# An attention, Fourier and feed-forward kernel: the first layer of the feed-forward over 512 tokens at once, the inner width in two halves

## The chip, the cores and the metric

The kernel runs on one core of one Trainium2 chip. The metric is the device time of one execution in microseconds (us), lower is better; the figure given for a kernel is the median of several runs. Engines are called PE (TensorE, matmuls), DVE (VectorE), ACT (ScalarE), POOL (GpSimd) and SP (SyncE, which issues the transfers).

## The reference

Eight batches, eight heads, 576 tokens, head width 64, so 512 channels; the inner width of the feed-forward is 2048.

```python
scores = q @ k.T / 8                                   # per batch and head, 576 x 576
scores = where(0 <= i - j < 128, scores - slope[h] * abs(i - j), -1e9)
x = softmax(scores) @ v                                # heads joined: (8, 576, 512)
mixed = real(fft(fft(x, axis=1), axis=2))              # over tokens, then channels
u = x + mixed
un = (u - mean(u)) / sqrt(var(u) + 1e-6)               # over channels
out = u + relu(un @ w_ch1) @ w_ch2                     # 512 -> 2048 -> 512
```

## The kernel before, in words

One function records the whole program. Every step is a small closure that is put into a heap, `queue`, at a planned time (`put`, or `after` for a time relative to the step that runs now); a last loop takes them out in the order of these times and records their instructions. The constants at the top (L44 to L60) are such times, in units in which a batch takes 24 and a pair of heads 6. A scheduler behind the recording then fixes the final order on each engine from the tiles' dependences and the buffers. A batch has four pairs of heads, so there are 32 pairs, called the first to the 32nd here.

**Attention.** For a pair, `scores` (L406) multiplies the keys by the queries into `sp` banks (L422). A float16 product is done as three: high by high, low by high, high by low, and 64 rows of TensorE are used by one head, the other 64 by the other head. DVE adds bias and mask from the scaled table `rg` (L434) and takes the row's largest value; ACT takes the exponential (L183, as all steps put by `after` carry the line of its lambda). Batches 0 and 1 (`NF` = 2) stay in float32: `turn` transposes P on TensorE (L466) and `values` multiplies (L488). Later batches split P in a high and a low half (`halves`, L448) and transpose it by a DMA (`flip`, L457), and `values` takes three products (L493 to L495). `weigh` divides by the row sums into `X` (L507 to L511). `warm` (L340, L342) records dummy matmuls that nobody reads, `SPL[p]` of them after each turn of pair p, and `N0` at the start (L338).

**Scales.** `batch_scales` (L274) loads a batch's q, k and v once more to find its scales, and makes the table `rg` = scale x `rel_sb` (L317, ACT, 128 x 1152, two buffers).

**Fourier.** `fourier(b, ...)` folds the rows of `X` (L555 to L604, DVE and ACT), multiplies by the cosine and sine tables over tokens (L619), then over channels (L637, L655), and `norm` (L715) normalizes, splits `un` in two float16 halves and transposes each token tile into `uT` with a DMA (`turned`, L749). `uT` holds two token tiles of 128 tokens, in three buffers; a batch has four full token tiles in two of them, and 64 tokens more, which for two batches together make one tile `ut`.

**Feed-forward.** `ffn(b)` (L765) is a generator; `step` (L835) runs it from one `yield` to the next at planned times, beginning at `forward_of(b)`. It goes over parts: two of two token tiles (256 columns), and in odd batches the `ut` tile (128 columns). A part runs the whole first layer: two inner groups f of 128 at a time share one 512-column bank `fp`, each with 12 matmuls (four channel groups, three products; L783). ACT takes the Relu into the high half of `hbuf` (L788), DVE the rest into the low half (`lower`, L758), which gives the bank back. Then the second layer (L799): for each token tile 48 matmuls of 512 columns (16 groups f, three products), and `joined` (L762) adds the result to `X` on DVE; the tile is sent out. Banks for `fp` come from `take` (two of three in turn, all three once `late` is set). The first weight, w1, and the second, w2, are split at the start by `weights` (L192, L245 to L249) into `wall`.

Of the kernel before, what the change touches and what calls it, by code (L numbers as in the profile page):

```python
# [43 lines left out]
LB, LC = 2, 5.046  # L44
E0 = 17.576
W1A, N0 = 1.058, 20
WL = (-2.569, 0.042)
PL, VL = 8.703, 2.996
PQ, T2, DF1, ST1, F1 = 0.911, 0.0, 29.452, 49.362, 0.9
SPL = (5, 6, 5, 5, 1, 1, 1, 1)  # L50
FL, SA, SD, SB, SE = 2.073, 16.745, 0.696, 24.163, 1.152
DFT = 29.394
START = 48.566
PACE, T1 = (0.443, 0.427), 13.679
GAP = 0.73
SLOW = 1.386
W2A, W2D, W2B, W2E = 16.635, 0.564, 21.18, 0.402
W1D, W1B, W1E = 0.379, 11.323, 0.508
F0 = 6.021
# [24 lines left out]
def attn_fft_ffn_kernel(  # L84
# [189 lines left out]
    def batch_scales(b, t0, dt):  # L274
# [28 lines left out]
        def scale():  # L303
            r = small.tile([128, 3], F32, name="r")
            root_inv(r, box["sums"])
            give(("scale", b))
            sc = small.tile([128, 8], F32, name="sc", bufs=3)
            V.tensor_scalar_mul(sc[:, 0:1], r[:, 0:1], 2.0 ** -58)
            V.tensor_scalar_mul(sc[:, 1:3], r[:, 1:3], 2.0 ** -51)
            V.scalar_tensor_tensor(sc[:, 3:4], sc[:, 0:1], 8.0, sc[:, 1:2], ALU.mult, ALU.mult)  # L310
            gi = small.tile([128, 8], F32, name="gi")
            V.reciprocal(gi[:, 0:1], sc[:, 3:4])
            nsl = small.tile([128, 12], F32, name="nsl")
            V.tensor_scalar(nsl[:, 0:8], slope_sb[:, 0:8], gi[:, 0:1], None, ALU.mult)
            V.tensor_scalar(nsl[:, 8:12], slope_sb[:, 8:12], sc[:, 0:1], None, ALU.mult)
            rg = att.tile([128, 1152], BF16, name="rg", bufs=2)
            A.activation(rg, rel_sb, AF.Copy, scale=sc[:, 3:4])  # L317
            x_scales(sc, gi, r[:, 2:3])
            scs[b] = sc, nsl, rg
# [54 lines left out]
    def convert(p, what):  # L374
# [7 lines left out]
        sc, nsl, rg = scs[b]  # L382
# [23 lines left out]
    def scores(p, i):  # L406
# [19 lines left out]
        for e in range(2):  # L426
            h = 2 * j + e
            nb = small.tile([128, 5], F32, name="nb", bufs=6)
# [30 lines left out]
    def turn(p, i, e):  # L459
# [11 lines left out]
        after(GAP, warm, upper, SPL[p])  # L471
# [243 lines left out]
    def norm(b, of, t1):  # L715
        tiles = of()
        n = len(tiles)
        if n == 2:
            uT = dft.tile([128, 2, 4, 256], F16, name="uT", bufs=3)
        else:  # L720
            assert (1, 7) in ready
            uT = wall[1][:, 8, 0:512].bitcast(F16).rearrange("p (e c t) -> p e c t", e=2, c=4)
        uTs[b].append(uT)
        ag = small.tile([128, 4, 2], F32, name="ag")
# [12 lines left out]
        def scaled(i):  # L737
# [7 lines left out]
            after(0.5 * f, turned, dst, both)  # L745

        def turned(dst, both):
            ready.add((b, id(uT)))
            nc.sync.dma_start_transpose(dst, both)  # L749
# [15 lines left out]
    def ffn(b):  # L765
# [3 lines left out]
        parts = [(uTs[b][i], 256, [X[:, XS[2 * i]], X[:, XS[2 * i + 1]]], 4 * b + 2 * i) for i in range(2)]  # L769
        if b % 2 == 1:  # L770
            parts.append((uTs[b][2], 128, [uts[b // 2]], 4 * B + b // 2))
        for uT, n, tiles, slot in parts:
            per = 512 // n
            hh = []
            assert (b, id(uT)) in ready
            for f0 in range(0, 16, per):
# [3 lines left out]
                for i in range(per):  # L780
# [4 lines left out]
                    if i == per // 2 - 1:  # L785
                        yield
# [3 lines left out]
                for i in range(per):  # L790
                    hh.append(ht[:, :, i * n:(i + 1) * n])
                yield
            for i, t in enumerate(tiles):
                key = ("second", b, slot, i)
                op = take(key, "fp")
                for f in range(16):
                    assert (1, f // 2) in ready
                    for p, (a, e) in enumerate(((0, 0), (0, 1), (1, 0))):
                        T.matmul(op, hh[f][:, a, i * 128:(i + 1) * 128], w2_ap(e, f),  # L799
                                 start=(f == 0 and p == 0), stop=(f == 15 and p == 2))  # L800
                    if f % 2 == 1 and f < 15:
                        yield
                after(0.15, joined, key, t, op)
                after(0.4, nc.sync.dma_start, out=ov[slot + i], in_=t)
# [162 lines left out]
```

## Time and profile before

| | us |
|---|---|
| median of 3 runs | 1052.02 |
| lowest and highest | 1051.59, 1053.05 |
| the profiled execution, whole | 1052.83 |
| its span, first to last instruction | 1051.0 |
| PE busy | 1027.8 |
| DVE busy | 701.1 |
| ACT busy | 582.2 |

The profile shows one execution. Busy time of an engine is the time in which it had an instruction at work; idle time is put down to whatever released the engine afterwards. [...] In rows of the timeline a run of like instructions is one row with its count (x24), and consecutive matmuls overlap, so a row's length is a little more than the distance to the start of the next.

### The profile page before, as it was taken

The page shows a single profiled execution, that of the slowest core. Times are in us where ns is not written, and L with a number is a line of the kernel's source. Part 1 is how long each engine was busy: PE and PEld are TensorE (multiplying, and loading weights), DVE is VectorE, ACT ScalarE, POOL GpSimd, SP SyncE. Part 2 cuts the span into 40 slices and gives each one's busy share as a digit, 9 for nine tenths or more (in the row PEclk, how much of TensorE's full clock was granted, in tenths as well). Part 3 has the DMA queues.
Part 4 walks back from the last instruction along what each step waited for, and adds up shares of the span by engine and source line. Part 5 has one row for each costly group of instructions (what it writes and reads, how often), then busy time and mean ns, then how long its engine had stood idle before and what let it go on. Part 6 is the DMA issues. An engine that isn't in the chain of part 4 may idle for free.

```text
span 1051.0 us, 24075 instructions
## 1 busy us (share of the span) xinstructions
PE 1027.8 (98%) x9214; PEld 721.6 (69%) x9214; DVE 701.1 (67%) x2073; ACT 582.2 (55%) x1388; POOL 77.4 (7%) x211
## 2 busy tenths in 40 slices
PE   8998999999999999999999999999999999999998
PEld 5885785575758677676767676776667775857656
DVE  5889769878676858696875858696866726532111
ACT  6887877667556646676555656665545512331100
POOL 0000003101010002110010012110000000000000
PEclk9996989999999999999999999999999999999999
DMA  9971356927752554636762475637322410030000
GB/s 365 357 237 37 106 125 171 206 64 145 172 132 67 135 116 117 154 71 143 167 144 54 110 151 116 157 67 155 72 64 34 91 35 11 12 70 1 21 11 21
DMA packets 191507, 117.82 MB, mean 112 GB/s; under 512 B 154400, under 2 KB 164128, under 8 KB 191392
## 3 DMA queue, kind: packets, MB, share of 16 engines
q1 hardware_dynamic: 190816, 114.84, 44.9%
q8 instruction: 72, 1.18, 0.5%
q10 hardware_dynamic: 576, 1.45, 0.4%
q14 instruction: 43, 0.35, 0.1%
HBM read 70.63 MB, written 9.44 MB: 76 GB/s over the span
## 4 chain that ended last, share of the span: by engine, by line
PE 83%; DVE 8%; DMA 3%; ACT 3%; issue 2%; POOL 0%; SPq 0%; ACTq 0%; DVEq 0%; POOLq 0%
PE fp L799 32%; PE fp L783 31%; PE sp L422 6%; PE pv L488 3%; PE pd L619 3%; DMA pt<-P 2%; DVE P L434 1%; PE sp L466 1%; PE pv L342 1%; PE pv L493 1%; PE pd L655 1%; PE pv L495 1%; PE pv L494 1%; DVE hbuf L758 1%; PE fp L225 1%
## 5 line engine op out<-in xcount | busy, mean ns | idle before, releaser
L799 PE MATMUL fp<-wall,hbuf 128*128 128x512 f16 x1728 | 393.2, 379 | 0.7 <-DVE hbuf L758 0.7
L783 PEld LDWEIGHTS <-wall 128*128 128x128 f16 x3840 | 337.6, 98 | 43.1 <-issue 4.3
L783 PE MATMUL fp<-uT,wall 128*128 128x256 f16 x3072 | 358.3, 273 | 0.4 <-DVE hbuf L758 0.4
L799 PEld LDWEIGHTS <-hbuf 128*128 128x128 f16 x1728 | 162.9, 98 | 183.2 <-issue 3.7
L788 ACT ACTIVATE hbuf<-fp 128x512 f16<-128x512 f32 x144 | 84.3, 589 | 194.0 <-PE fp L783 194.0
L183 ACT ACTIVATE P<-P,nb 128x256 f32<-128x256 f32 x320 | 142.0, 479 | 79.6 <-DVE nb L434 79.1
L758 DVE SCALAR_TENSOR_TENSOR hbuf<-fp,hbuf 128x512 f16<-128x512 f32 x144 | 98.4, 685 | 87.9 <-ACT hbuf L788 87.2
L434 DVE CUSTOM_DVE_ANT_0 P<-sp,rg,nsl 128x256 f32<-128x256 f32 x240 | 97.4, 449 | 26.2 <-PE sp L422 24.7
L183 DVE SCALAR_TENSOR_TENSOR P<-P 128x256 f16<-128x256 f32 x240 | 88.9, 390 | 31.9 <-ACT P L448 29.7
L448 ACT ACTIVATE P<-P 128x256 f16<-128x256 f32 x240 | 86.7, 382 | 14.0 <-DMA pt<-P 11.5
L422 PE MATMUL sp<-kk,qq 64*128 64x256 f16 (+4 forms) x880 | 89.1, 289 | 1.5 <-DVE m L173 1.0
L296 ACT ACTIVATE wall<-wall 128x512 f32<-128x512 f32 (+2 forms) x90 | 54.1, 602 | 22.2 <-POOL mx L295 6.6
L762 DVE SCALAR_TENSOR_TENSOR X<-fp,misc,X 128x512 f32<-128x512 f32 x32 | 23.7, 742 | 54.1 <-PE fp L799 54.1
L288 POOL COPY wall<-nb 1x1 f32<-1x1 f32 x75 | 34.2, 459 | 339.0 <-DVE nb L434 225.1
L493 PE MATMUL pv<-vhs,pt 128*128 128x65 f16 x432 | 54.1, 195 | 4.7 <-DMA pt<-P 2.5
L494 PE MATMUL pv<-vl,pt 128*128 128x64 f16 x432 | 54.2, 193 | 0.0
L495 PE MATMUL pv<-vhs,pt 128*128 128x65 f16 x432 | 53.7, 193 | 0.0
L493 PEld LDWEIGHTS <-pt 128*128 128x128 f16 x432 | 41.0, 98 | 14.2 <-issue 4.1
L422 PEld LDWEIGHTS <-qq 64*128 64x128 f16 (+1 forms) x720 | 29.9, 99 | 24.1 <-issue 18.8
L494 PEld LDWEIGHTS <-pt 128*128 128x128 f16 x432 | 40.4, 99 | 7.3
L783 PE MATMUL fp<-wall,wall 128*128 128x128 f16 x768 | 45.0, 219 | 0.0
L488 PEld LDWEIGHTS pv<-vr,pt 128*128 128x128 f32 x288 | 39.1, 207 | 7.3 <-PE pv L342 4.2
(160 smaller groups left out, 1231.5 us busy)
## 6 DMA issues: line engine op xcount, KB each, us to landing
qr<-q_dram SPq DMA_DIRECT2D x32, 304.0 KB, 3.3
hbuf<-w_dram SPq DMA_DIRECT2D x16, 512.0 KB, 7.1
out_dram<-X SPq DMA_DIRECT2D x32, 256.0 KB, 2.5
wall<-v_dram SPq DMA_DIRECT2D x30, 256.0 KB, 2.9
vr<-v_dram SPq DMA_DIRECT2D x24, 320.0 KB, 3.8
kr<-k_dram SPq DMA_DIRECT2D x24, 289.0 KB, 3.5
wall<-q_dram SPq DMA_DIRECT2D x24, 256.0 KB, 3.1
wall<-k_dram SPq DMA_DIRECT2D x24, 256.0 KB, 2.9
```

Source lines behind the costliest of these rows:

```text
L183: put(now[0] + dt, lambda: f(*a, **kw))
L422: T.matmul(sp[e][:m, col:col + n], qq[h, c0:c0 + m], keys(kk[h], ti), start=(x == 0), stop=(x == len(prods) - 1))
L434: V.tensor_tensor_reduce(pt[:m, 0:n], sp[e][:m, col:col + n], tab[:m, pc:pc + n], mul, 3.0e38, ALU.add, ALU.min, nb[:m, ti:ti + 1])
L448: A.activation(hi, P32, AF.Copy, scale=2.0 ** 14)
L488: T.matmul(pv[:, ti], pt[:, col:col + 128], ops[p][2][:, e, vc], start=first, stop=last)
L493: T.matmul(pv[:, ti], ph, vh[:, e, vc], start=first, stop=False)
L494: T.matmul(pv[:, ti, 0:D], ph, vl[:, e, vc], start=False, stop=False)
L495: T.matmul(pv[:, ti], pl, vh[:, e, vc], start=False, stop=last)
L758: V.scalar_tensor_tensor(ht[:, 1], fp, 0.0, ht[:, 0], ALU.max, ALU.subtract)
L783: T.matmul(fp[:, i * n:(i + 1) * n], w1_ap(e, c, f0 + i), uT[:, j, c, 0:n], start=(c == 0 and p == 0), stop=(c == 3 and p == 2))
L788: A.activation(ht[:, 0], fp, AF.Relu)
L799: T.matmul(op, hh[f][:, a, i * 128:(i + 1) * 128], w2_ap(e, f), start=(f == 0 and p == 0), stop=(f == 15 and p == 2))
```

## The change

Three things. First, the first layer of a batch takes all four token tiles at once, so one inner group f fills a 512-column bank by itself, in 12 matmuls of 512 columns. `uT` now has 512 columns and two buffers, and the first layer needs all four transposed tiles. Second, the inner width is halved: eight groups f go through the first layer and then, for all four tiles, through the second (24 matmuls a tile), and then the other eight. Each token tile is therefore added into `X` twice, and sent out after the second time. The part of 128 columns stays as it was. Third, the table `rg` is made by a step of its own just before the batch's first scores and has one buffer. Besides, `nb` has four buffers instead of six, the count of dummies is given for each turn, and the planned times are set anew.

```diff
@@ -41,22 +41,23 @@
 TGRP = ((0, 1), (2, 3), (4,))
 
 
-LB, LC = 2, 5.046
-E0 = 17.576
-W1A, N0 = 1.058, 20
-WL = (-2.569, 0.042)
-PL, VL = 8.703, 2.996
-PQ, T2, DF1, ST1, F1 = 0.911, 0.0, 29.452, 49.362, 0.9
-SPL = (5, 6, 5, 5, 1, 1, 1, 1)
-FL, SA, SD, SB, SE = 2.073, 16.745, 0.696, 24.163, 1.152
-DFT = 29.394
+LB, LC = 2, 5.066
+E0 = 7.777
+W1A, N0 = 1.854, 21
+WL = (-2.569, 0.408)
+PL, VL = 7.761, 2.996
+PQ, T2, DF1, ST1, F1 = 0.754, -0.085, 28.727, 45.662, 0.9
+SPL = ((5, 2, 6, 7, 5, 5), (6, 6, 6, 6, 6, 6), (5, 5, 5, 4, 5, 5), (3, 5, 5, 5, 5, 5), (3, 1, 1, 1, 1, 1), (1, 1, 1, 0, 1, 1), (2, 1, 1, 1, 0, 2), (1, 1, 1, 3, 1, 0))
+RG = 0.2
+FL, SA, SD, SB, SE = 2.073, 16.545, 0.661, 23.561, 1.211
+DFT = 29.51
 START = 48.566
-PACE, T1 = (0.443, 0.427), 13.679
+PACE, T1 = (0.443, 0.497), 13.94
 GAP = 0.73
-SLOW = 1.386
-W2A, W2D, W2B, W2E = 16.635, 0.564, 21.18, 0.402
-W1D, W1B, W1E = 0.379, 11.323, 0.508
-F0 = 6.021
+SLOW = 1.35
+W2A, W2D, W2B, W2E = 16.635, 0.584, 20.304, 0.402
+W1D, W1B, W1E = 0.362, 11.211, 0.508
+F0 = 10.277
 SW = 184
 
 
@@ -313,10 +314,15 @@
             nsl = small.tile([128, 12], F32, name="nsl")
             V.tensor_scalar(nsl[:, 0:8], slope_sb[:, 0:8], gi[:, 0:1], None, ALU.mult)
             V.tensor_scalar(nsl[:, 8:12], slope_sb[:, 8:12], sc[:, 0:1], None, ALU.mult)
-            rg = att.tile([128, 1152], BF16, name="rg", bufs=2)
-            A.activation(rg, rel_sb, AF.Copy, scale=sc[:, 3:4])
             x_scales(sc, gi, r[:, 2:3])
-            scs[b] = sc, nsl, rg
+            scs[b] = sc, nsl
+
+        def table():
+            rg = att.tile([128, 1152], BF16, name="rg", bufs=1)
+            A.activation(rg, rel_sb, AF.Copy, scale=scs[b][0][:, 3:4])
+            scs[b] += rg,
+
+        put(begin_of(4 * b) - RG, table)
 
         put(t0 - 2.5 * dt, begin)
         x = 0
...
@@ -468,7 +474,7 @@
         pt = pts[p, i, e] = att.tile([128, 448], F32, name="pt", bufs=6)
         A.activation(pt[:, :col], tp[:, :col], AF.Copy)
         upper = pt.bitcast(BF16).rearrange("p (x e) -> p x e", e=2)[:, :, 1]
-        after(GAP, warm, upper, SPL[p])
+        after(GAP, warm, upper, SPL[p][2 * i + e])
 
     def values(p, i, e):
         b, j = divmod(p, 4)
@@ -715,12 +721,17 @@
     def norm(b, of, t1):
         tiles = of()
         n = len(tiles)
-        if n == 2:
-            uT = dft.tile([128, 2, 4, 256], F16, name="uT", bufs=3)
-        else:
+        o = 256 * len(uTs[b])
+        if n == 1:
             assert (1, 7) in ready
             uT = wall[1][:, 8, 0:512].bitcast(F16).rearrange("p (e c t) -> p e c t", e=2, c=4)
+        elif o:
+            uT = uTs[b][0]
+        else:
+            uT = dft.tile([128, 2, 4, 512], F16, name="uT", bufs=2)
         uTs[b].append(uT)
+        if n == 2:
+            uT = uT[:, :, :, o:o + 256]
         ag = small.tile([128, 4, 2], F32, name="ag")
         rstd = small.tile([128, 4], F32, name="rstd")
         nmr = small.tile([128, 4], F32, name="nmr")
@@ -742,10 +753,10 @@
             A.activation(both[:, 0:512], tiles[i], AF.Identity, scale=s, bias=o)
             after(0.3 * f, V.tensor_tensor, both[:, 512:1024], un, both[:, 0:512], ALU.subtract)
             dst = uT[:, :, :, i * 128:(i + 1) * 128].rearrange("p e c t -> p (e c) t")
-            after(0.5 * f, turned, dst, both)
-
-        def turned(dst, both):
-            ready.add((b, id(uT)))
+            after(0.5 * f, turned, dst, both, i)
+
+        def turned(dst, both, i):
+            ready.add((b, o, i))
             nc.sync.dma_start_transpose(dst, both)
 
         for i in range(n):
@@ -766,14 +777,16 @@
         if b:
             late.append(b)
         X = Xs[b]
-        parts = [(uTs[b][i], 256, [X[:, XS[2 * i]], X[:, XS[2 * i + 1]]], 4 * b + 2 * i) for i in range(2)]
+        parts = [(uTs[b][0], 512, [X[:, i] for i in XS], 4 * b, h) for h in range(2)]
         if b % 2 == 1:
-            parts.append((uTs[b][2], 128, [uts[b // 2]], 4 * B + b // 2))
-        for uT, n, tiles, slot in parts:
+            parts.append((uTs[b][2], 128, [uts[b // 2]], 4 * B + b // 2, None))
+        for uT, n, tiles, slot, h in parts:
             per = 512 // n
-            hh = []
-            assert (b, id(uT)) in ready
-            for f0 in range(0, 16, per):
+            fs = range(16) if h is None else range(8 * h, 8 * h + 8)
+            hh = {}
+            for o, i in ((0, 0), (0, 1), (256, 0), (256, 1)) if n == 512 else ((512, 0), ):
+                assert (b, o, i) in ready
+            for f0 in fs[::per]:
                 assert (0, (f0 + per - 1) // 2) in ready
                 key = ("first", b, slot, f0)
                 fp = take(key, "fp")
@@ -782,26 +795,27 @@
                         for p, (e, j) in enumerate(((0, 0), (0, 1), (1, 0))):
                             T.matmul(fp[:, i * n:(i + 1) * n], w1_ap(e, c, f0 + i), uT[:, j, c, 0:n],
                                      start=(c == 0 and p == 0), stop=(c == 3 and p == 2))
-                    if i == per // 2 - 1:
-                        yield
+                        if (i * 4 + c + 1) * 2 == per * 4:
+                            yield
                 ht = next(hslots)
                 A.activation(ht[:, 0], fp, AF.Relu)
                 after(0.2, lower, key, ht, fp)
                 for i in range(per):
-                    hh.append(ht[:, :, i * n:(i + 1) * n])
+                    hh[f0 + i] = ht[:, :, i * n:(i + 1) * n]
                 yield
             for i, t in enumerate(tiles):
-                key = ("second", b, slot, i)
+                key = ("second", b, slot, i, h)
                 op = take(key, "fp")
-                for f in range(16):
+                for f in fs:
                     assert (1, f // 2) in ready
                     for p, (a, e) in enumerate(((0, 0), (0, 1), (1, 0))):
                         T.matmul(op, hh[f][:, a, i * 128:(i + 1) * 128], w2_ap(e, f),
-                                 start=(f == 0 and p == 0), stop=(f == 15 and p == 2))
-                    if f % 2 == 1 and f < 15:
+                                 start=(f == fs[0] and p == 0), stop=(f == fs[-1] and p == 2))
+                    if f % 2 == 1 and f != fs[-1]:
                         yield
                 after(0.15, joined, key, t, op)
-                after(0.4, nc.sync.dma_start, out=ov[slot + i], in_=t)
+                if h != 0:
+                    after(0.4, nc.sync.dma_start, out=ov[slot + i], in_=t)
                 yield
```

The order of the instructions on each engine follows from the planned times. At three places it now reads as follows. In the rows, `vr`, `qq`, `kk` are the values, queries and keys of a pair, `pt` the transposed P, `wall` the weights, `hbuf` the inner activations, `fh` and `abcd` the folded rows of the Fourier step.

PE where the feed-forward of batch 0 begins, before:

```order
L342 LDWEIGHTS pt
L342 MATMUL pv<-pt 128x184
L488 MATMUL pv<-vr,pt 128x65 x2
L466 MATMUL sp_2157<-ident,P 128x128 x2
L783 LDWEIGHTS wall_112
L783 MATMUL fp<-uT,wall_112 128x256
```

and now:

```order
L494 MATMUL pv<-vr,pt 128x65 x2
L472 MATMUL sp_2042<-ident,P 128x128 x2
...
L494 MATMUL pv<-vr,pt 128x65 x3
...
L494 MATMUL pv<-vr,pt 128x65 x4
L348 LDWEIGHTS pt
L348 MATMUL pv<-pt 128x184
L494 MATMUL pv<-vr,pt 128x65 x2
L796 LDWEIGHTS wall_112
L796 MATMUL fp<-uT,wall_112 128x512
```

A turn (L466, now L472) stood directly ahead of the feed-forward; now nine more value matmuls and dummies (L348) stand between the two.

DVE about the first score step of the ninth pair (L434, now L440), before, where the fold of batch 1 begins some 40 rows further on:

```order
L511 TENSOR_TENSOR X<-pv,ri 128x5x64
L249 SCALAR_TENSOR_TENSOR wall_113<-wall_113,misc 128x1024
L267 TENSOR_SCALAR sc<-m_2109 128x1
L758 SCALAR_TENSOR_TENSOR hbuf<-fp,hbuf 128x512
L434 ISA P,nb<-sp_2173,rg,nsl 128x256
```

and now:

```order
L582 TENSOR_TENSOR abcd<-pm 128x2x128 x2
...
L561 TENSOR_TENSOR fg<-X 128x512
...
L769 SCALAR_TENSOR_TENSOR hbuf<-fp,hbuf 128x512
...
L610 SCALAR_TENSOR_TENSOR fl_2409<-abcd,sc,fh_2366 128x512
...
L571 TENSOR_TENSOR pm<-fg 128x2x256
...
L184 SCALAR_TENSOR_TENSOR kk<-kr,sc,kk 128x578
...
L440 ISA P,nb<-sp_2087,rg,nsl 128x256
```

The fold of batch 1 (L561 to L610) now stands ahead of that pair's first score step, among the `lower` steps (L769) of the first layer of batch 0.

PE in a later batch, now, where a run of scores (L428, before L422) is cut by a Fourier row and has three matmuls of one head and then three of the other:

```order
L812 MATMUL fp<-wall_113,hbuf 128x512
L428 LDWEIGHTS qq
L428 MATMUL sp_2261<-kk,qq 128x256
...
L625 LDWEIGHTS fh_2426
L625 MATMUL pd<-tab_sb,fh_2426 128x289
L428 LDWEIGHTS qq
L428 MATMUL sp_2262<-kk,qq 128x256
...
L812 LDWEIGHTS hbuf
```

`sp_2261` and `sp_2262` are the two heads' banks; such score runs were 87 in the six float16 batches and are now 110.

## Rows read from the trace of the kernel before

**Rows 1.** The page, busy time of the engines in us, share of the span and instructions.

```profile
PE 1027.8 (98%) x9214; PEld 721.6 (69%) x9214; DVE 701.1 (67%) x2073; ACT 582.2 (55%) x1388; POOL 77.4 (7%) x211
```

**Rows 2.** The table by stage: start and end in us, length, busy time and instructions of PE, of its weight loads, of DVE, ACT and POOL, the granted clock, the share of the DMA engines and GB/s.

```profile
85.70:106.20 20.50, 19.32 (x71) 12.88 (x72) 18.07 (x54) 14.22 (x27) 0.10 (x1) 0.50 0.08 25
133.50:140.40 6.90, 6.90 (x36) 5.84 (x36) 5.07 (x13) 6.77 (x12) 0.61 (x1) 0.51 1.16 216
150.00:300.00 150.00, 141.64 (x1291) 95.89 (x1289) 125.55 (x389) 103.23 (x248) 21.06 (x54) 1.00 0.63 140
300.00:850.00 550.00, 549.43 (x5344) 381.51 (x5343) 399.61 (x1191) 320.89 (x798) 49.40 (x130) 1.00 0.50 110
```

**Rows 3.** What PE waited for from 150 us to the end: its line, then the engine and line waited for, us in all, times, the longest.

```profile
PE pv L493 <- DMA pt<-P: 2.5, 2, 1.6
PE pv L493 <- DVE X L511: 2.2, 2, 1.6
PE pd L619 <- DVE zl L627: 1.2, 1, 1.2
PE sp L422 <- DVE m L173: 1.0, 1, 1.0
PE pd L619 <- ACT fh L592: 0.8, 1, 0.8
PE fp L799 <- DVE hbuf L758: 0.7, 1, 0.7
PE fp L783 <- DVE hbuf L758: 0.4, 2, 0.2
```

**Rows 4.** PE's timeline in the tail: start, length, operation.

```profile
921.93 20.88 PE L799 MATMUL fp<-wall,hbuf 128*128 128x512 f16 x96
942.65 21.12 PE L783 MATMUL fp<-uT,wall 128*128 128x256 f16 x192
963.61 20.88 PE L799 MATMUL fp<-wall,hbuf 128*128 128x512 f16 x96
```

**Rows 5.** The page, costliest groups: line, engine, operation, out<-in, shapes, count, busy us, mean ns of one, idle time before and what ended it.

```profile
L783 PE MATMUL fp<-uT,wall 128*128 128x256 f16 x3072 | 358.3, 273 | 0.4 <-DVE hbuf L758 0.4
L788 ACT ACTIVATE hbuf<-fp 128x512 f16<-128x512 f32 x144 | 84.3, 589 | 194.0 <-PE fp L783 194.0
L758 DVE SCALAR_TENSOR_TENSOR hbuf<-fp,hbuf 128x512 f16<-128x512 f32 x144 | 98.4, 685 | 87.9 <-ACT hbuf L788 87.2
L762 DVE SCALAR_TENSOR_TENSOR X<-fp,misc,X 128x512 f32<-128x512 f32 x32 | 23.7, 742 | 54.1 <-PE fp L799 54.1
```

**Rows 6.** PE's timeline about runs of scores (L422), columns as in rows 4; in brackets the idle time before and what ended it.

```profile
158.40 1.11 PE L422 MATMUL sp<-kk,qq 64*128 64x256 f16 x20 [1.03 <-DVE m L173]
159.45 2.79 PE L783 MATMUL fp<-uT,wall 128*128 128x256 f16 x24
...
168.00 5.34 PE L799 MATMUL fp<-wall,hbuf 128*128 128x512 f16 x24 [0.67 <-DVE hbuf L758]
173.27 0.68 PE L422 MATMUL sp<-kk,qq 64*128 64x256 f16 x12
...
434.62 0.28 PE L422 MATMUL sp<-kk,qq 64*128 64x256 f16 x1
434.84 0.30 PE L619 MATMUL pd<-tab_sb,fh 128*128 128x289 f16 x1
...
470.72 0.50 PE L422 MATMUL sp<-kk,qq 64*128 64x256 f16 x3
471.15 0.82 PE L799 MATMUL fp<-wall,hbuf 128*128 128x512 f16 x3
```

**Rows 7.** PE's timeline before and at the start of the feed-forward of batch 0.

```profile
125.17 0.88 PE L488 MATMUL pv<-vr,pt 128*128 128x65 f32 x6
...
127.44 0.70 PE L422 MATMUL sp<-kk,qq 64*128 64x256 f32 x2
...
137.09 7.02 PE L783 MATMUL fp<-uT,wall 128*128 128x256 f16 x48
143.94 0.24 PE L342 MATMUL pv<-pt 128*128 128x184 bf16 x1
```

**Rows 8.** The timelines of DVE and of SP's queue, where the last two token tiles of batch 0 are subtracted (L183) and transposed (L749).

```profile
137.73 1.28 DVE L183 TENSOR_TENSOR un<-un 128x512 f16<-128x512 f32 x2
...
138.44 3.57 SPq L749 DMA_TRANSPOSE uT<-un  x2
```

**Rows 9.** The instructions of L749, the transposes into `uT`.

```profile
DMA to landing us min/median/max: 2.7/3.2/5.2
```

**Rows 10.** DVE's timeline: the first score step of the ninth pair, and the first and last large step of the fold of batch 1.

```profile
161.31 0.47 DVE L434 CUSTOM_DVE_ANT_0 P<-sp,rg,nsl 128x256 f32<-128x256 f32 x1
...
176.54 0.67 DVE L555 TENSOR_TENSOR fg<-X 128x512 f32<-128x512 f32 x1
...
200.31 0.74 DVE L604 SCALAR_TENSOR_TENSOR fl<-abcd,sc,fh 128x512 f16<-128x512 f32 x1
```

**Rows 11.** The table by stage, columns as in rows 2.

```profile
140.00:250.00 110.00, 104.78 (x965) 73.31 (x964) 92.30 (x285) 79.34 (x191) 17.99 (x43) 1.00 0.60 134
180.00:200.00 20.00, 18.58 (x141) 10.15 (x139) 19.67 (x66) 15.13 (x40) 2.61 (x11) 1.00 0.87 197
```

**Rows 12.** The groups by line: the scaled table.

```profile
L317 ACT ACTIVATE rg<-rel_sb,sc 128x1152 bf16<-128x1152 bf16 x6 | 7.4, 1240 | 0.0
```

More of the change, by code (lines that the diff above doesn't have):

```diff
@@ L381, in convert @@
             return
-        sc, nsl, rg = scs[b]
+        sc, nsl = scs[b][:2]
         if what < 2:
@@ L427, in scores @@
             h = 2 * j + e
-            nb = small.tile([128, 5], F32, name="nb", bufs=6)
+            nb = small.tile([128, 5], F32, name="nb", bufs=4)
             col = 0
```

## The prediction, made before the changed kernel had run

> **What bounds the kernel now.** I read the page's engine totals first [rows 1]: TensorE (PE) is busy 1027.8 of 1051.0 us, 98%, while VectorE (DVE) has 67% and ScalarE (ACT) 55%. A change can therefore save time in three places only: less PE work, the 23.2 us in which PE stands idle, and the stretches in which PE runs at half clock. Next the table by stage [rows 2], which shows what the totals hide: from 300 to 850 us PE is busy 549.43 of 550 with DVE at 399.61, so nothing but PE's own work counts there. [...] Then the waits of PE [rows 3]: after 150 us they sum to 8.8 us, of which only 1.1 belong to the feed-forward itself (hbuf L758); the rest are attention and fourier steps waiting for DVE, ACT or the DMA transposes. A change of 0.2%, 2.1 us, is about what a measurement of this kernel can tell from none.
>
> The profiled execution took 1052.83 us, 0.8 over the median of 1052.02; I sum against the former and take 0.8 off at the end.
>
> **First layer in 512 columns.** The cleanest prices stand in the tail, where only the FFN is left [rows 4]: 192 first-layer matmuls of 256 columns take 963.61 - 942.65 = 20.96 us, 109.2 ns each, and 96 of 512 columns take 942.65 - 921.93 = 20.72 us, 215.8 ns each. Two of 256 become one of 512, which saves (20.96 - 20.72)/96 = 2.5 ns; times 1536 (half of x3072 [rows 5]) that is **-3.8 us**. That is all that the wider matmul brings; the columns are the same. The 768 matmuls of 128 columns stay. [...]
>
> **Score runs cut up.** The scores (L422) are matmuls with 64 rows, issued in runs between the FFN's. Ten pairs of 256 columns take 1.05 us (158.40 to 159.45 [rows 6]), 105 ns a pair, two heads side by side. A single one takes 0.22 us (434.62 to 434.84), so about 0.11 is fixed at the end of a run; and 24 second-layer matmuls ahead of a run take 5.27 us (168.00 to 173.27) against 24 x 215.8 ns = 5.18, so 0.09 to 0.10 at its start. In the new order other work stands between heads more often: counting its rows, 87 runs of the float16 batches become 110, and 32 matmuls without a partner from the other head become 46. 23 x 0.206 + 14 x 0.05 = **+5.4 us**. Lower end: 0.11 a cut, 2.5 us. Upper end: three unpaired take 0.43 us (470.72 to 471.15 [rows 6]), as long as three pairs would (3 x 0.105 + 0.11), so a cut that parts three pairs costs 0.43 more, 23 x 0.43 = 9.9. [...]
>
> **FFN(0) starts later.** Its first matmul now needs all four transposed tiles, not two. Before, it began at 137.09 us [rows 7]; the last two `un` tiles are only subtracted on DVE at 137.73 to 139.0, their transposes issue from 138.44, and a transpose lands 3.2 us after its issue (median) [rows 8, 9]. The fourth, issued within that row of 3.57 us, at about 140, lands near 143.5: 6.4 us later. Against this stand values of the eighth pair and some dummies that the new order puts ahead of the FFN, like the 2.3 us from 125.17 to 127.44 [rows 7]; and the first 48 FFN matmuls, which ran partly at half clock (137.09 to 143.94, 6.85 us against 5.24 at 109.2 ns each), lose that penalty of 1.6. 6.4 - 2.3 - 1.6 = **+2.5 us**; ends 0 (all covered by moved work) and +6.4.
>
> **Waits from 150 to 300 us.** Two things in the new order bear on them. The fold of batch 1 (in the trace at 176.54 to 200.31 us, among the first float16 scores [rows 10]) now stands on DVE ahead of the first score step of the ninth pair, under FFN(0)'s first layer; and 10 to 15 us more FFN work stands ahead of the scores of pairs 9 to 16, by the order's counts. DVE, at 19.67 of 20 us between 180 and 200 [rows 11], is relieved where the waits are. I take away all waits but the FFN's own: 8.8 - 1.1 = **-7.7 us**. Ends: -8.8, and 0 if each is replaced.
>
> **Half the inner width at a time.** A second-layer tile now starts after 8 groups of the inner width, so the last hbuf of a half must be ready after 7 x 3 = 21 matmuls, 4.5 us, where it had 42, 9 us. Relu and subtraction alone take 0.59 + 0.69 us [rows 5], and with queueing several us. Before, 20 such starts cost 1.1 us of waits [rows 3]; I double it: **+1.1 us**, ends 0 and 10.7 (16 starts at the 0.67 of 168.00 [rows 6]). The 32 added adds on DVE, 742 ns each [rows 5], make 23.7 us in all, 3.0 per batch. In the steady stretch DVE has 150 us free of 550, so they cost nothing there; without that cover they would stand in front of the score steps, which is the second rival.
>
> **Table made late, and the boundary at pair 17.** The scaled table (ACT, 1.24 us [rows 12]) has one buffer and is made just before its batch's first scores, which wait for it only if ACT is late. At the batch boundary ahead of pair 17 the order leaves about 5 us of FFN work between two pairs' scores where 20 stood, so one value step may wait for its DMA transpose, as two did for up to 1.6 us [rows 3]. I take half of one: **+0.8 us**, ends 0 and 4.8 (three steps).
>
> **Sum.** -3.8 + 5.4 + 2.5 - 7.7 + 1.1 + 0.8 = -1.7: 1051.1 for the profiled execution, **1050.3 us** for the median. In the steady part it is slightly worse; the start decides.
>
> **Rivals.**
> *Faster, the start is covered.* FFN(0)'s late start is filled with moved work (term at 0: -2.5), a cut of the scores costs only its 0.11 (-2.9), and half of the slow stretch about FFN(0)'s beginning goes (6.9 us at 0.51 [rows 2], half of its 3.4 lost us: -1.7): 1050.3 - 7.1 = **1043.2**. For it: that stretch and the 20.5 us at half clock from 85.7 us [rows 2] leave room. Against: from batch 0's first fourier row on, the order in the slow stretch from 90 to 106 us is unchanged.
> *Slower, DVE in 140 to 250 us.* DVE is busy 92.3 of 110 us there [rows 11]. If the fold, now ahead of the scores, makes the ninth pair's first score step late by more than the FFN filler covers, the waits stay (+7.7 against the sum): **1058.0**; with batch 0's four added adds exposed too (3.0), 1061.0. It decides if the ninth pair's first score step on DVE comes more than about 12 us (the added FFN work) after the 161.31 [rows 10] of before. ACT is part of it: by the order seven Relus, not four, stand ahead of that pair's scaled queries.
> *Far faster, long matmuls overlap.* If a 512-column matmul took no longer than one of 256 because its end overlaps the next one's start, 1536 x 109.2 ns = 168 us would go: 884 at the most. The 512-column rows of this kernel [rows 4] speak against it and leave it 1 in 100. [...]
> That the change does not do what it says is excluded by the order: 1536 first-layer matmuls of 512 columns are there.
>
> **Chances.** Forecast 0.45, with a range of its own of 1046 to 1054 (faster 0.21, same 0.22, slower 0.02); faster rival 0.21; slower rival 0.33 (slower 0.30, same 0.03); overlap 0.01. Faster 0.43, same 0.25, slower 0.32. The range, 1042 to 1061, leaves out what lies beyond the two rivals, some 0.08 on each side.
>
> **What would show it.** First-layer matmuls of 512 columns at 215 to 216 ns in the tail; scores some 5 us dearer between 160 and 850; FFN(0)'s first matmul at 142 to 145 us; PE waits of 1 to 3 us after 150, none on P or m of pairs 9 to 16; PE still over 99% busy from 300 to 850. The prediction is wrong if FFN(0) starts before 140, if the waits of 150 to 300 exceed 6 us, or if 300 to 850 holds waits on hbuf or rg.

## The result, and the profile after

| | before | after |
|---|---|---|
| median, us | 1052.11 (1051.59 to 1053.05, 4 runs) | 1063.06 (1062.66 to 1063.22, 4 runs) |
| profiled execution: span, us | 1051.0 | 1061.4 |
| mean granted clock | 0.985 | 0.977 |

The change is slower: ratio 1.0102, 95% interval 1.0087 to 1.0118, so 11 us where 2 us faster was forecast and the range ended at 1061. The page's totals come first. The sum of PE's busy time answers to [rows 1]:

```profile
PE 1038.4 (98%) x7679; PEld 576.7 (54%) x7679; DVE 723.7 (68%) x2105; ACT 581.3 (55%) x1388; POOL 73.3 (7%) x211
```

PE is busy 10.6 us longer and idle as long as before (23.0 us, before 23.2). So the loss isn't a new wait on the whole: PE takes longer for its work. The table by stage of the changed kernel says why (columns as in [rows 2]; the first four stretches are those in which half of TensorE's full clock was granted):

```profile
13.30:23.60 10.30, 10.24 (x53) 8.46 (x52) 5.15 (x14) 7.87 (x18) 0.00 (x0) 0.50 1.04 402
88.40:108.90 20.50, 18.72 (x70) 12.35 (x69) 18.83 (x58) 14.89 (x28) 0.10 (x1) 0.50 0.12 37
136.20:149.90 13.70, 12.66 (x53) 9.49 (x53) 7.84 (x18) 10.61 (x19) 0.81 (x2) 0.50 0.84 196
378.60:382.00 3.40, 3.32 (x8) 1.20 (x9) 3.40 (x13) 2.06 (x5) 0.00 (x0) 0.50 0.47 93
...
150.00:300.00 150.00, 145.20 (x1018) 72.57 (x1017) 117.80 (x347) 97.65 (x231) 18.74 (x50) 1.00 0.59 132
300.00:850.00 550.00, 546.37 (x4453) 293.96 (x4452) 421.70 (x1249) 326.14 (x814) 48.98 (x137) 1.00 0.52 112
```

The kernel before has three such stretches; two of them are in [rows 2], the first is

```profile
14.00:17.50 3.50, 3.33 (x22) 3.20 (x23) 2.14 (x7) 3.50 (x9) 0.00 (x0) 0.51 1.04 411
```

PE's work at half clock is 3.33 + 19.32 + 6.90 = 29.6 us before and 10.24 + 18.72 + 12.66 + 3.32 = 44.9 us after. In the feed-forward of the changed kernel one 512-column matmul starts 427 ns after another in such a stretch, and 216 ns outside. So at full clock the work would take about half, and by this estimate the clock costs 14.8 us before and 22.5 after: **7.7 of the 10.6 us** of PE's added time. The other 2.9 us is PE work at full clock: -3.8 for the columns, the others for cut score runs and what lies about them. (The 8.5 us of e1's expectation counts the whole lengths of the stretches.) The 300 to 850 us stretch, which answers to the last of [rows 2], now has 3.6 us of idle where it had 0.6.

What the first slow stretch costs can be read from four profiles in which the order on PE, DVE and ACT is the same up to 130 us: the changed kernel, the changed kernel run again (e13 below), and e14 and e7, whose edits act later. The stretch lasted 10.2, 6.8, 3.4 and 0 us. The same four score matmuls start the later, the longer it was (PE's timelines, in this order):

```profile
87.80 1.06 PE L428 MATMUL sp<-kk,qq 64*128 64x256 f32 x4 [0.79 <-ACT pt L475]
85.95 0.92 PE L428 MATMUL sp<-kk,qq 64*128 64x256 f32 x4 [0.79 <-ACT pt L475]
84.52 0.92 PE L428 MATMUL sp<-kk,qq 64*128 64x256 f32 x4 [0.79 <-ACT pt L475]
83.78 0.92 PE L428 MATMUL sp<-kk,qq 64*128 64x256 f32 x4 [0.79 <-ACT pt L475]
```

So 10.2 us of it cost 3.3 us more than 3.4 us, and its length differs between executions of one and the same kernel. Then PE's wait for `X` ahead of FFN(0): it ends at 132.72 us in the kernel before and at 135.44 in the changed one. So 2.7 of the 10.4 us of span are lost before the feed-forward begins.

```profile
132.72 0.24 PE L342 MATMUL pv<-pt 128*128 128x184 bf16 x1 [3.22 <-DVE X L511]
```

PE's timeline at the start of FFN(0) [rows 7] and in the tail [rows 4], in the changed kernel:

```profile
135.44 0.32 PE L348 MATMUL pv<-pt 128*128 128x184 bf16 x2 [2.84 <-DVE X L517]
...
140.80 0.31 PE L348 MATMUL pv<-pt 128*128 128x184 bf16 x1 [0.58 <-DMA wall<-v_dram]
...
146.19 7.15 PE L796 MATMUL fp<-uT,wall 128*128 128x512 f16 x24 [0.40 <-DMA uT<-un]
```

```profile
953.50 20.88 PE L796 MATMUL fp<-uT,wall 128*128 128x512 f16 x96
974.23 20.88 PE L812 MATMUL fp<-wall,hbuf 128*128 128x512 f16 x96
994.95 20.88 PE L796 MATMUL fp<-uT,wall 128*128 128x512 f16 x96
```

FFN(0) begins at 146.19 us, 9.1 later than before: 2.7 us of that are the loss at the start, and from the wait for `X` on it comes after 10.75 us where it came after 4.37, so 6.4 later. Its first 24 matmuls take about 7 us for 5.2 of full clock. In the tail a first layer of 96 matmuls takes 974.23 - 953.50 = 20.73 us and a second layer 20.72: 215.9 ns each, as forecast. PE's waits from 150 us to the end [rows 3]:

```profile
PE fp L796 <- DMA uT<-un: 2.7, 1, 2.7
PE fp L812 <- ACT P L454: 2.5, 1, 2.5
PE sp L428 <- DVE qq L184: 0.8, 1, 0.8
PE pv L499 <- DMA pt<-P: 0.7, 1, 0.7
PE pd L625 <- DVE zl L633: 0.7, 1, 0.7
PE fp L796 <- DVE hbuf L769: 0.5, 2, 0.3
PE fp L812 <- DVE hbuf L769: 0.3, 1, 0.3
```

The attention and Fourier steps, which had 7.7 us of these waits, have 2.2. But the feed-forward's own went from 1.1 to 6.0: 2.7 us in which batch 1's first layer waits for its four transposed tiles, and 2.5 of the second layer, put down to P of L454. There ACT had stood still for 2.36 us, to 374.43, until a transpose into `uT` was done with `un`; the Relu (377.24) and its low half on DVE (377.85 to 378.54) stand behind that in the order, and PE went on at 378.68. That PE needed these two is the likely reading. Last the float16 scores by shape, before and then after (busy us, mean ns of one):

```profile
L422 PE MATMUL sp<-kk,qq 64*128 64x256 f16 x432 | 40.0, 274 | 1.0 <-DVE m L173 1.0
L422 PE MATMUL sp<-kk,qq 64*96 64x256 f16 x144 | 12.2, 271 | 0.0
L422 PE MATMUL sp<-kk,qq 64*128 64x128 f16 x144 | 8.5, 217 | 0.0
```

```profile
L428 PE MATMUL sp<-kk,qq 64*128 64x256 f16 x432 | 42.8, 274 | 0.8 <-DVE qq L184 0.8
L428 PE MATMUL sp<-kk,qq 64*96 64x256 f16 x144 | 13.8, 275 | 0.0
L428 PE MATMUL sp<-kk,qq 64*128 64x128 f16 x144 | 9.6, 217 | 0.0
```

60.7 us became 66.2: +5.5. Rows overlap their neighbours, so this is no exact price. Counted from the start of one matmul to the start of the next, at full clock, the float16 scores take 46.8 us before and 50.1 after; a second-layer matmul directly ahead of a run of scores takes 312 ns (median) where the others take 216. With 0.1 us for each of 23 more runs that makes 5.6 us. And the first score step of the ninth pair on DVE [rows 10] comes 20 us later, while PE waits only 0.8 us for a score's operand ([rows 3] had 1.0):

```profile
181.24 0.48 DVE L440 CUSTOM_DVE_ANT_0 P<-sp,rg,nsl 128x256 f32<-128x256 f32 x1
```

### The profile page after: what moved, and what is told of

Its sections match the earlier page's. It is cut to its first block, busy times and chain, and to the rows that moved or that the text cites. A ratio compares the mean times of both kernels' runs of the same rounds, so it can differ in the third digit from the quotient of the medians.

```text
span 1061.4 us, 21036 instructions
## 1 busy us (share of the span) xinstructions
PE 1038.4 (98%) x7679; PEld 576.7 (54%) x7679; DVE 723.7 (68%) x2105; ACT 581.3 (55%) x1388; POOL 73.3 (7%) x211
## 4 chain that ended last, share of the span: by engine, by line
PE 78%; DVE 11%; ACT 5%; DMA 4%; issue 2%; POOL 0%; SPq 0%; DVEq 0%; ACTq 0%
PE fp L796 30%; PE fp L812 30%; PE sp L428 5%; PE pd L625 2%; PE pv L494 2%; DMA uT<-un 1%; PE pd L661 1%; DVE P L440 1%; PE pv L499 1%; PE pv L348 1%; PE sp L472 1%; PE pv L500 1%; PE pv L501 1%; DMA pt<-P 1%; ACT P L184 1%
## 5 line engine op out<-in xcount | busy, mean ns | idle before, releaser
L796 PE MATMUL fp<-uT,wall 128*128 128x512 f16 x1536 | 353.2, 381 | 3.5 <-DMA uT<-un 3.1
L796 PEld LDWEIGHTS <-wall 128*128 128x128 f16 x2304 | 187.2, 98 | 168.9 <-issue 8.7
L769 DVE SCALAR_TENSOR_TENSOR hbuf<-fp,hbuf 128x512 f16<-128x512 f32 x144 | 98.6, 686 | 85.6 <-ACT hbuf L801 84.9
L440 DVE CUSTOM_DVE_ANT_0 P<-sp,rg,nsl 128x256 f32<-128x256 f32 x240 | 97.9, 450 | 35.4 <-PE sp L428 29.9
L428 PE MATMUL sp<-kk,qq 64*128 64x256 f16 (+4 forms) x880 | 95.6, 291 | 2.0 <-ACT pt L475 1.0
L454 ACT ACTIVATE P<-P 128x256 f16<-128x256 f32 x240 | 86.3, 383 | 4.8 <-DMA pt<-P 4.1
L773 DVE SCALAR_TENSOR_TENSOR X<-fp,misc,X 128x512 f32<-128x512 f32 x64 | 47.6, 744 | 57.3 <-PE fp L812 57.2
L289 POOL COPY wall<-nb 1x1 f32<-1x1 f32 x75 | 30.9, 412 | 358.1 <-DVE nb L440 186.0
L428 PEld LDWEIGHTS <-qq 64*128 64x128 f16 (+1 forms) x720 | 29.9, 99 | 31.7 <-issue 25.3
L494 PE MATMUL pv<-vr,pt 128*128 128x65 f32 x288 | 46.1, 306 | 0.5 <-ACT pt L475 0.3
L494 PEld LDWEIGHTS pv<-vr,pt 128*128 128x128 f32 x288 | 42.7, 223 | 5.5 <-PE pv L348 2.4
```

The source lines that it names most:

```text
L428: T.matmul(sp[e][:m, col:col + n], qq[h, c0:c0 + m], keys(kk[h], ti), start=(x == 0), stop=(x == len(prods) - 1))
L440: V.tensor_tensor_reduce(pt[:m, 0:n], sp[e][:m, col:col + n], tab[:m, pc:pc + n], mul, 3.0e38, ALU.add, ALU.min, nb[:m, ti:ti + 1])
L454: A.activation(hi, P32, AF.Copy, scale=2.0 ** 14)
L494: T.matmul(pv[:, ti], pt[:, col:col + 128], ops[p][2][:, e, vc], start=first, stop=last)
L769: V.scalar_tensor_tensor(ht[:, 1], fp, 0.0, ht[:, 0], ALU.max, ALU.subtract)
L796: T.matmul(fp[:, i * n:(i + 1) * n], w1_ap(e, c, f0 + i), uT[:, j, c, 0:n], start=(c == 0 and p == 0), stop=(c == 3 and p == 2))
```

## The experiments

Times are medians; beside them the ratio to the kernel before, run on the same chip (1052.7 to 1052.9 us). Theory A in the expectations is the clock (and, where said, cuts and waits), theory B the rival named there; theory C is told where it first stands. In e3 and e15 the first half of the inner width is missing from the output of the tiles that are halved.

| kernel | us | ratio, 95% interval |
|---|---|---|
| e1_start_times | 1066.3 | 1.0124 (1.0105 to 1.0142) |
| e2_swapped | 1055.9 | 1.0024 (1.0013 to 1.0035) |
| e3_no_first_adds | 1061.4 | 1.0084 (1.0065 to 1.0103) |
| e4_all_old_times | 1065.9 | 1.0127 (1.0110 to 1.0143) |
| e5_halves_256 | 1077.3 | 1.0238 (1.0202 to 1.0273) |
| e6_batch0_as_before | 1055.2 | 1.0029 (1.0013 to 1.0045) |
| e7_more_dummies | 1061.2 | 1.0075 (1.0049 to 1.0101) |
| e8_old_times_batch0 | 1065.2 | 1.0124 (1.0103 to 1.0145) |
| e9_fewer_cuts | 1064.8 | 1.0102 (1.0076 to 1.0129) |
| e10_batch0_fewer_cuts | 1057.3 | 1.0036 (1.0015 to 1.0056) |
| e11_two_batches_as_before | 1055.9 | 1.0025 (1.0015 to 1.0036) |
| e12_and_old_start | 1055.4 | 1.0023 (1.0008 to 1.0039) |
| e13_change_again | 1062.1 | 1.0094 (1.0073 to 1.0114) |
| e14_batch0_again | 1057.6 | 1.0050 (1.0031 to 1.0068) |
| e15_batch0_no_first_adds | 1055.0 | 1.0014 (0.9991 to 1.0037) |

**The late start of FFN(0).** e2_swapped puts it alone into the kernel before:

```diff
+        if b == 0:
+            parts.reverse()
```

> The kernel before, with the two parts of batch 0's feed-forward in swapped order, so that its first matmul waits for the last two token tiles instead of the first two; nothing else is changed. Theory A: FFN(0) begins at 143 to 147 us, the second slow stretch lasts 10 to 14 us instead of 6.8, since the clock rises only after the dense feed-forward begins, and the time is 1055 to 1058. Theory B (the late start is covered by the values that move ahead, as the prediction had it in part): FFN(0) begins as late, but the time stays at 1051 to 1053.5.

Measured: 0.24% or 2.5 us slower (1.4 to 3.7). FFN(0) began at 143.4 us and the second slow stretch was as long as the changed kernel's. The table by stage, and PE's timeline:

```profile
133.30:147.00 13.70, 12.29 (x60) 10.47 (x60) 7.45 (x19) 10.62 (x19) 0.87 (x2) 0.50 0.84 187
```

```profile
143.39 7.16 PE L785 MATMUL fp<-uT,wall 128*128 128x256 f16 x48 [0.77 <-DMA uT<-un]
```

Theory A in kind; the size is at the lower end. FFN(0) begins 10.75 us after the wait for `X` (132.64), as in the changed kernel, and 3.4 us more at half clock followed a wait of 2.02 us at 168. e6_batch0_as_before takes the late start out of the change, and with it the halves, the wide first layer and the four added adds of batch 0; e13 and e14 repeat the change and e6 side by side:

```diff
+        if b == 0:
+            parts = [(uTs[0][0][:, :, :, 256 * i:256 * i + 256], 256, [X[:, XS[2 * i]], X[:, XS[2 * i + 1]]], 2 * i, None)
+                     for i in range(2)]
```

> The changed kernel with batch 0's feed-forward in two parts of 256 columns as before, so that it begins with the first two tiles; the rest as in the change. Theory A (the late start of FFN(0) costs by the clock, as e2_swapped measured on before, 3.2 us): FFN(0) begins near 140 us, the second slow stretch is 6.8 us instead of 13.7, time 1059 to 1061. Theory B (the late start is no part of the loss here): 1062.5 to 1064.

> The changed kernel itself once more, beside e14 on one chip. If the late FFN(0) is the cause of the 7.8 us: 1062 to 1064, a first slow stretch of 10.2 us or less, the second of 13.7. If the first slow stretch, which differs between runs, made much of it: 1058 to 1062.

> e6_batch0_as_before itself once more, beside e13. If the late FFN(0) is the cause: 7 to 8 us under e13 (1054.5 to 1056), the second slow stretch 6.8 us. If the first slow stretch made much of it: 3 to 5.5 us under e13.

Measured: 0.73% less than the change in the first pair of runs, 0.44% in the second, 7.7 and 4.6 us. e6 is below what both theories expected, and e14 falls where its expectation gives a part to the first slow stretch. The profiles bear that out: e6 is 8.0 us shorter than the change and e14 6.6 shorter than e13, but measured from the four score matmuls above (85.84 in e6) it is 6.0 and 5.2. So batch 0's feed-forward as a whole makes about half of the loss; how much of that is the late start alone only e2 shows, in the kernel before. In e14 the second slow stretch (table by stage) is as before, and the feed-forward's waits come to 3.3 us, where e13 has 5.4 (2.7 of them on `uT`):

```profile
133.90:140.70 6.80, 6.80 (x35) 5.19 (x35) 4.77 (x10) 6.60 (x13) 0.00 (x0) 0.50 1.02 200
```

```profile
PE fp L815 <- ACT P L454: 2.3, 1, 2.3
PE fp L799 <- DVE hbuf L769: 0.4, 1, 0.4
PE fp L815 <- DVE hbuf L769: 0.3, 1, 0.3
PE fp L799 <- DVE m L173: 0.3, 1, 0.3
```

e7_more_dummies asks whether denser work ahead of FFN(0) brings the clock back: `SPL` of the eighth pair is 10 after each turn.

```diff
-..., (1, 1, 1, 3, 1, 0))
+..., (10, 10, 10, 10, 10, 10))
```

> The changed kernel with 10 dummies after each turn of the eighth pair instead of 0 to 3, some 24 more ahead of FFN(0). Theory A (the clock comes back only behind dense work): the slow stretch about 136 us falls from 13.7 to 6.8 or 10.2 us, which gives 1.7 to 3.4 back, and 24 dummies at 0.1 us take 2.4: 1061.5 to 1064. Theory B (the clock does not follow the dummies): the stretch stays at 13.7, the dummies at half clock cost 0.16 us each: 1064.5 to 1067.

Measured: 1061.2, from 1056.0 to 1063.1 in six runs, so some 2 us may be won, and that is not certain. The profiled execution is the fastest of the six: it had no first slow stretch and was 4.0 us ahead at the four score matmuls, which the dummies, coming later, didn't do. In its rows the slow stretch ended at 134.4 us, 0.3 us into the second of two groups of ten dummies, and a new one began at 137.9, after PE had waited 1.82 us. The two parts together are as long as the one was, 13.6 us for 13.7. Table by stage, then PE's timeline:

```profile
127.60:134.40 6.80, 5.26 (x28) 4.81 (x28) 4.91 (x19) 6.39 (x13) 0.69 (x1) 0.50 0.65 149
137.90:144.70 6.80, 5.98 (x21) 2.69 (x20) 2.42 (x2) 3.02 (x7) 0.17 (x1) 0.50 0.74 205
```

```profile
130.94 1.74 PE L348 MATMUL pv<-pt 128*128 128x184 bf16 x10
...
134.13 1.13 PE L348 MATMUL pv<-pt 128*128 128x184 bf16 x10
...
137.72 1.61 PE L348 MATMUL pv<-pt 128*128 128x184 bf16 x10 [1.82 <-DVE X L517]
140.16 7.13 PE L796 MATMUL fp<-uT,wall 128*128 128x512 f16 x22 [0.82 <-DMA uT<-un]
```

**The planned times.** e1 gives the change the start constants of before, e4 all planned times of before, e8 those and batch 0's old feed-forward.

```diff
-W1A, N0 = 1.854, 21
-WL = (-2.569, 0.408)
+W1A, N0 = 1.058, 20
+WL = (-2.569, 0.042)
...
```

> The changed kernel with the start constants of before alone (W1A, N0, WL and the dummies SPL per pair). Theory A, the clock: of the 10.4 us lost, 8.5 are the longer half clock, and 3.4 of these lie at the very start, where the first slow stretch lasted 10.2 us instead of 3.4 because weight conversion and dummies stand otherwise. Then the first slow stretch is back at 3.4 us and the time is 1059.6 (1058.8 to 1060.6). Theory B, the structure: the loss is in the batches, the start makes up for it; the time stays within 1 us of 1063.1.

> The structure of the changed kernel (512 columns, two halves, late table) with all planned times and dummies of before. Theory A: start as in e1_start_times, FFN(0) late all the same, score runs cut as often (103 runs, 68 unpaired, 0.5 us cheaper than in the change): 1058.5 to 1060.5, so timing constants explain a third of the loss and the structure the rest. Theory B: new times were needed by the structure, without them waits on PE grow: over 1064.

> All planned times of before, and batch 0's feed-forward as before; the new structure (512 columns, halves, late table) in batches 1 to 7 only. Against e4_all_old_times it takes away the late FFN(0). Theory A: 3.2 us less than e4_all_old_times, 1062 to 1063.5; the rest against before is cut scores (102 runs, 62 unpaired: 4.6 us), waits on uT and hbuf (5 to 8), less 3.4 for 512 columns. Theory C: most of the loss of e4_all_old_times hangs on FFN(0): 1054 to 1057.

Measured: 1066.3, 1065.9 and 1065.2, by the ratios 0.2 to 0.3% over the change, at the edge of the intervals. e8 missed both theories. In e1 the first slow stretch was 3.4 us as theory A said, but PE's idle time grew by 7 us (one wait of values alone 4.2) and two slow stretches of 3.4 us came after 177 us: its time is a miss. With the old times the structure loses some 13 us, and the new times seem to win back 2 to 3 of them; PE is idle for 28.1 us in e4 and for 23.0 in the change. With the old times it makes little difference how FFN(0) begins: the slow stretch about 135 us is 13.7 us in e4 and 6.8 in e8, but PE is idle for 29.6 us in e8, and 6.8 us at half clock follow at 260. But with the change's start constants the first slow stretch was 3.4 us too (e9, e11, e14, e15), or 6.8 (e6, e13), or 10.2 (e3, e10), or absent (e7), and with those of before 6.8 in e4 and e12: that it follows these constants is not shown.

**Halves, adds and cuts.** e5 has halves alone, in batches 1 to 7, with 256 columns and all else as before.

```diff
-        parts = [(uTs[b][i], 256, ..., 4 * b + 2 * i) for i in range(2)]
+        parts = [(uTs[b][i], 256, ..., 4 * b + 2 * i, h)
+                 for i in range(2) for h in (range(2) if b else (None,))]
...
```

> The kernel before with the inner width in halves in batches 1 to 7 (28 added adds), but 256 columns as before and two tiles at a time; batch 0, the table and all times as before. By the order 95 score runs and 88 unpaired matmuls instead of 87 and 32, 4.2 us dearer by the prediction's prices. Theory A (halving costs by cut scores and by waits on hbuf): 1058 to 1061 with 2 to 4 us more PE waits on hbuf. Theory C (halving costs by cut scores alone, the waits come from needing four tiles): 1056 to 1057.5 and waits on hbuf as before. If the adds and cuts cost nothing: 1052 to 1053.

Measured: 1077.3, far over every expectation. From 300 to 850 us PE is busy only 536.22 of 550 us. PE's waits are mostly on DVE (5.5 us for the second layer put down to a Fourier step, 3.0 on hbuf, 4.0 for values). At two tiles a half has half the work of PE to cover its DVE steps; that this is why, and that four tiles at once make halves bearable, fits but was not tried apart from the times.

e3 and e15 leave out the added adds, in the change and in e6.

```diff
-                after(0.15, joined, key, t, op)
+                after(0.15, *((give, key) if h == 0 else (joined, key, t, op)))
```

> The changed kernel without the 32 added adds: the result of the first half of the inner width is left out of the output in each tile. Theory A with the adds on the path: the adds delay DVE's score steps, and the order without them has 100 score runs instead of 110 and 30 unpaired matmuls instead of 46, 3.0 us cheaper by the prediction's prices: 1060.1 (1058.5 to 1061). Theory B, the adds are hidden as predicted: 1062.5 to 1063.5.

> e14 without the 28 added adds of batches 1 to 7: the first half of the inner width is left out of those tiles' output. By the order 100 score runs and 32 unpaired matmuls instead of 109 and 42, 2.4 us cheaper by the prediction's prices. Theory A (the adds cost through cut score runs, 1.7 in e3): 1.5 to 2.5 us under e14. Theory B (waits take their place, as in e9): within 1 us of e14.

Measured: e3 is 0.10% to 0.18% under the change (e13 and its first runs), 1 to 2 us, and e15 0.36% under e14, 3.8 us, by the medians 2.6; with these intervals the sign is likely in e15 and open in e3, and the size is not settled. In the traces the float16 scores fall from 66.2 to 62.4 us (e3) and from 65.9 to 63.1 (e15). The adds are 32 x 0.74 us on an engine that is idle a third of the time. By the order the scores come in 100 runs without them and in 110 with them, so the likely way is that the adds delay the score steps behind them on DVE, and the scores are issued in more pieces.

e9 takes cuts away by one planned time.

```diff
-START = 48.566
+START = 48.3
```

> The changed kernel with one planned time moved, START 48.566 to 48.3 (the feed-forward of batches 2 to 7 begins 1.4 us earlier against the attention). By the order the score runs are 98 instead of 110 and the unpaired matmuls 30 instead of 46, 3.2 us cheaper by the prediction's prices; the start and FFN(0) are untouched. If the cuts cost what was priced: float16 scores, second layer and values together 3 us lower in the trace and 1059 to 1060.5. If cuts are hidden or waits take their place: 1062.5 to 1064.

Measured: 1064.8 us, no gain. The scores by shape, and PE's waits from 150 us on:

```profile
L428 PE MATMUL sp<-kk,qq 64*128 64x256 f16 x432 | 40.9, 274 | 0.8 <-DVE qq L184 0.8
L428 PE MATMUL sp<-kk,qq 64*96 64x256 f16 x144 | 13.8, 274 | 0.0
L428 PE MATMUL sp<-kk,qq 64*128 64x128 f16 x144 | 9.6, 217 | 0.0
```

```profile
PE fp L796 <- DMA uT<-un: 3.5, 1, 3.5
PE fp L812 <- ACT P L454: 2.6, 1, 2.6
PE fp L812 <- DVE zl L633: 2.2, 2, 1.1
PE fp L796 <- DVE zl L633: 1.6, 1, 1.6
```

The scores fell by 1.9 us, to 64.3; with 0.1 us ahead of each of 12 runs fewer that is 3.1, so the price of 3.2 held, and PE's busy time fell by 3.1 too. But the waits rose from 8.2 to 12.5 us, and the whole idle time from 23.0 to 28.2. Up to 399 us the order is the changed kernel's; 3.2 of the 4.3 us of added waits stand behind that. In this run waits took the place of cuts, so the price of a cut is not what its removal wins. e10 to e12 put the parts together:

> e6_batch0_as_before with START 48.3: 97 runs, 26 unpaired, 3.2 us cheaper than e6 by the same prices. If late FFN(0) and cuts are separate terms: 1055.2 - 3.2 = 1052.0 (1051 to 1053.5), level with the kernel before. If not separate: 1054.5 to 1056.

> e10 with batch 1's feed-forward in two parts of 256 columns as well, 512 columns and halves from batch 2 on: 93 runs, 22 unpaired (0.7 us more than before), 8 added adds less. The wait of batch 1's first layer on uT (1.6 to 2.7 us) goes, the 512 columns lose 0.5 us more. If the terms are separate: 1050 to 1052, under the kernel before by 1 or 2 us. If waits come elsewhere: 1052 to 1055.

> e11 with the start constants of before (W1A, N0, WL, SPL), as in e1_start_times: 93 runs, 24 unpaired. The first slow stretch is 3.4 us instead of 6.8 to 10.2, 1.7 to 3.4 us less: 1047 to 1050 if no wait takes its place. If, as in e1, the later waits grow with it: 1051 to 1056.

Measured: 1057.3, 1055.9, 1055.4. The cuts were not won on top of batch 0: e10 lies between e6 and e14, though the first slow stretch of its profile, 10.2 us for 6.8 and 3.4, is part of that. In e11 the first layer's wait for the transposes went from 1.2 us in e10 to 0.4, and the values waited 3.4 us for theirs. No version tried beat the kernel before.

## Why the prediction was wrong

- **First layer in 512 columns**, -3.8: right, 20.73 us for what took 20.96, 215.9 ns for one matmul.
- **Score runs cut up**, +5.4: right, 5.6 from start to start (+5.5 of busy time in the rows). But it couldn't be had back: e9 got waits for it.
- **FFN(0) starts later**, +2.5: the first step that failed. The delay was right: 6.4 us, counted from the wait for `X`. The error is the clock. I booked 1.6 us as won, since FFN(0) would start behind the slow stretch. The rows show the reverse: in six profiles the slow stretch ended 3.3 to 4.5 us after FFN(0) had begun, wherever that was (137.1 and 140.4 before; 146.2 and 149.9 after; 143.4 and 147.0 in e2; 144.1 and 148.6 in e13; 136.4 and 140.7 in e14; 140.2 and 144.7 in e7). With the later start the stretch was longer: 13.7 us for 6.8, 12.66 us of PE work for 6.90, so 2.9 us lost in place of 1.6 won. The moved values and dummies, 2.3 us at full clock, ran in it and took 5.0 (140.80 to 145.8), so they covered most of the delay: PE was idle for 1.0 us in the stretch, where 6.4 - 2.3 had left 4.1. Clock and idle time together make 3.9. That e2 measured just the 2.5 of the term is luck, as two errors of opposite sign stand in it. In the change e6 and e14 win 4.6 to 7.7 us, but with the halves of batch 0, the waits that follow and the first slow stretch in the figure.
- **Waits from 150 to 300 us**, -7.7: in kind right, -5.5. They went as the order said.
- **Half the inner width**, +1.1: the second step that failed, in its size. The feed-forward's own waits rose by 4.9 us, inside the ends of 0 and 10.7; the largest, batch 1's first layer on `uT`, I had not named, though the four-tile rule that I priced for batch 0 holds for every batch. It isn't the rule alone: in e6 and e14 batch 1 needs four tiles as well, and no wait on `uT` stands in their rows after 150 us. So all waits after 150 us fell from 8.8 to 8.2 us, where three terms of the sum let them fall by 5.8. The sign of being wrong that was named for this, waits on hbuf from 300 to 850 us, came with 0.3 us and, by the likely reading above, the 2.5 us at 376. This wait was followed by a slow stretch of 3.4 us, 1.7 lost. The adds, booked at nothing, cost 1 to 2 us by e3, within its interval, and 2.6 to 3.8 by e15; by the order these are in part the cut score runs counted above.
- **Table and boundary**, +0.8: no wait on `rg`, and none at pair 17.
- Not in the sum: the first slow stretch, 10.2 us for 3.4 in these two profiles; 2.7 us were lost by the wait for `X`. In e13, the same kernel, it was 6.8. What sets it is open, so this part of the loss may be luck.
- **The sum of it**, an estimate from these rows: -1.7 was forecast for the span and +10.4 came, 12.1 apart. Of these the first slow stretch makes 2.7, FFN(0) 1.4, the slow stretch at 378 us 1.7 and the waits after 150 us 5.2. About 1 us has no row.
- **The rivals.** The slower one had the sign and not the mechanism: its trigger came (the ninth pair's score step 20 us later, over the 12), but the FFN work ahead covered it, and the attention waits went. The loss ran through the clock, which I had as a source of gain alone, and through new waits of the feed-forward. The time lies beyond both ends of this rival.

## What to carry to other kernels

A start that is moved must be priced with the clock that it leaves behind: here the slow stretch ended only 3.3 to 4.5 us after the feed-forward had begun, with 6.4 us of delay it was 6.8 us longer, and the 2.3 us of work moved into it took 5.0. A need for more finished inputs (four tiles for two) holds for every repetition, so look for its wait in all of them. Where PE is busy 98% of the time by a balance of planned times, terms for cuts and for waits need not add: in e9 taking the one away brought the other. And before two single profiles are compared, look for a place up to which their orders are the same: a difference in time there is not the change's.

## What the runs showed of the hardware

- From 126 us to the last matmul, every stretch at half clock in the profiles of before, the change, e2, e7, e13 and e14 came with a wait of PE of 1.8 to 3.2 us, but not every such wait brought one: in the changed kernel the 2.54 us at 376 us were followed by 3.4 us at 0.50, the 2.66 us at 258 us were not. The stretch that begins at 88.4 us there came with two short waits, 0.79 and 0.77 us.
- The first slow stretch lasted 0, 3.4, 6.8 or 10.2 us in ten profiles with the same order up to 130 us (the change, e3, e6, e7, e9 to e11, e13 to e15), and the same matmuls started at 83.78 us after 0 us of it (e7), at 84.52 after 3.4 (e14), at 85.95 after 6.8 (e13) and at 87.80 after 10.2 (the change).
- Runs of the same kernel differ in the clock. Of 17 runs of the kernel before beside e13, the one of 1047.7 us had a mean granted clock of 0.990 and the one of 1056.9 us 0.982, about 1 us for each 0.001. Differences under 2 us are not to be told from so few runs.
